# The second FFN of batches 2 to 7 as seven block products per 2x2 block, with weight sums read back from DRAM and VectorE held to the source's order

## The chip, the cores and the metric

The kernel runs on one core of one Trainium2 chip. The metric is the time of one execution on the device, in microseconds (us). In the profile PE is TensorE, which does the matrix products; PEld is its loading of the stationary operand; DVE is VectorE, ACT is ScalarE, POOL is GpSimd, and SP is SyncE, whose queue starts most DMAs. SBUF is the memory the engines compute from, PSUM the eight banks that PE writes its sums into, and DRAM the device's main memory.

## The reference, cut to what matters

Eight batches of 576 tokens go through an attention with 32 memory slots per head (8 heads of 64), and the result goes through a feed-forward network (FFN) of two large products. In all there are 4608 tokens, 512 model columns and 2048 hidden columns.

```python
a = softmax(phi)                                  # over the 32 slots
k_m = einsum('bhsm,bhsd->bhmd', a, k)             # and v_m likewise
attn = softmax(matmul(q, k_m.T) / sqrt(64))       # over the 32 slots
x = matmul(attn, v_m)  -> [4608, 512]
h = x @ w_in                                      # [4608, 2048]
g = h * (1.0 / (1.0 + np.exp(-h)))
return g @ w_out                                  # [4608, 512]
```

## The kernel before, in words

The first FFN is folded into the attention: `p_mm` (L592) multiplies `v_m` by `w_in` once per batch, 512 hidden columns at a time, and `ffn1` (L622) then multiplies that product by the attention weights. Every operand of the two large products is held as two parts, a rounded one and the rest of it (`hi` and `lo`), and each product is made of three: hi x hi, hi x lo and lo x hi.

**The loop.** For each batch `b` the main loop (L882) goes over 16 chunks `fc` of 128 hidden columns. One chunk is one slot. In a slot PE first does `ffn1`: twelve products with a moving operand of 288 tokens, into the PSUM tile `h`, which has one buffer. ACT applies silu to it (`silu`, L657): 512 tokens go into `g32`, and the 64 tokens left over go into `gleft`. DVE splits `g32` into `ghi` and `glo` (`split`, L646: a copy of 512 columns, then a subtraction of 512). Then come the events of this slot, and then `finish` (L874) does the second FFN of the slot before: `main_step` (L689) takes four tiles of 128 tokens, and for each of them `ffn2` (L671) does three products with a moving operand of 512 columns, which is all the model columns. So the order on PE is: first FFN of this slot, events of this slot, second FFN of the previous slot. Sums stay in the four `acc` banks for the whole batch and are copied out by `store` (L680) at its end. After every odd batch the left-over 64 tokens of two batches make one more tile of 128, done in four left steps (`left_step`, L695) of twelve products of 512 columns.

**The events** are the attention of the next batch `n`, spread over the slots of batch `b` by the tuple `at_slot` (L718), and the four `p_mm` of a batch. In the order of the tuple: `phi_max`; `phi_fold` and, half a slot later, `phi_sub`; `phi_exp`; `e_mm` (96 small products; half a slot or a slot from it the loads of `kv` and `q`); `e_tr`; `s_all` (scores, then transposes on DVE, of which two read columns beside `h`); `s_max` and `s_sub`; `s_exp`; `s_sum`; `s_norm`; `s_back` and `s_low` (the attention weights in two parts) with the load of the next `phi`. Each `p_mm` is followed by a copy on ACT and a subtraction on DVE (`p_split`, L612).

**What sets the order.** The context manager `in_order` (L98) ties each instruction of an engine to the one before it in the source. It holds PE throughout (L764), ACT from batch 1 on (L885), and SP in the opening and batch 0. DVE in batches 1 to 7 is placed by the scheduler of the framework.

Weights: `w_out` stands in SBUF as `wo_hi` and `wo_lo`, 16 chunks of 128 rows by 512 columns. `raw` is a pool of three buffers, through which weights come in and outputs go out; `cva` and `cva1` are two buffers that the weight conversion of batch 0 uses.

Of the kernel before, what the change touches and what calls it, by code (L numbers as in the profile page):

```python
# [48 lines left out]
def attn_ffn_kernel(  # L49
# [10 lines left out]
    const = ctx.enter_context(tc.tile_pool(name="const", bufs=1))  # L60
    sb = ctx.enter_context(tc.tile_pool(name="sb", bufs=2))
    ps = ctx.enter_context(tc.tile_pool(name="ps", bufs=1, space=bass.MemoryType.PSUM))

    kvn = const.tile([P, 2, 2, D], F32, name="kvn")
    ident = const.tile([P, P], F32, name="ident")
# [174 lines left out]
    def phi_max(b, ps_=(0, 1)):  # L240
        e, er = at[b]["e"], at[b]["er"]
        g = slice(ps_[0], ps_[-1] + 1)
        if "mx" not in at[b]:
            at[b]["mx"] = sb.tile([P, 2, P], F32, tag="mx", name="mx", bufs=1)
            at[b]["mt"] = sb.tile([P, 2, 2, P], F32, tag="g32", name="mt", bufs=2)
        mx, mt = at[b]["mx"], at[b]["mt"]
        nc.vector.tensor_tensor(mt[:, g], e[:, g, 0:2], e[:, g, 2:4], op=ALU.max)
        nc.vector.tensor_tensor(mx[:, g], mt[:, g, 0], mt[:, g, 1], op=ALU.max)
        for p in ps_:
            nc.vector.tensor_tensor(mx[rows(p), p], mx[rows(p), p], er[rows(p)], op=ALU.max)  # L250
# [62 lines left out]

    def e_mm(b):
        e, er, kvt, kr = (at[b][k] for k in ("e", "er", "kv", "kr"))
        pt = banks(b) if b < 2 else beside_h(KVW)
        turns = [(c, p) for c in range(FULLC) for p in range(2)]
        if b == 0:
            turns.sort(key=lambda t: t[1])
        for c, p in turns:  # L320
            for r in range(NR):
                nc.tensor.matmul(  # L322
                    pt[p][M * r : M * (r + 1), :KVW],
                    e[:, p, c, M * r : M * (r + 1)],
                    kvt[c][:, p, r],
                    start=c == 0, stop=False, skip_group_check=True,
                )
        for r in range(NR):
            for p in range(2):
                nc.tensor.matmul(  # L330
                    pt[p][M * r : M * (r + 1), :KVW],
                    er[rows(p), M * r : M * (r + 1)],
                    kr[rows(p), r],
                    start=False, stop=True, skip_group_check=True,
                )
        rs = [sb.tile([P, 1], F32, tag="rs", name="rs", bufs=2) for p in range(2)]
        for p in range(2):
            nc.vector.tensor_scalar(rs[p], pt[p][:, 2 * D : KVW], EPS, None, op0=ALU.add)
        for p in range(2):
            nc.vector.reciprocal(rs[p], rs[p])  # L340
        for p in range(2):
            src = pt[p][:, : 2 * D].rearrange("p (k d) -> p k d", k=2)
            if p == (b == 0):
                nc.scalar.activation(kvn[:, :, p], src, AF.Copy, scale=rs[p])
            else:
                nc.vector.tensor_scalar(kvn[:, :, p], src, rs[p], None, op0=ALU.mult)

    def e_tr(b):
        pt = beside_h(P)
        t = sb.tile([P, 2, NR, M], F32, tag="kvT", name=f"kvT{b}", bufs=2)  # L350
        for kind in range(2):
            nc.tensor.transpose(pt[kind], kvn[:, kind].rearrange("p g d -> p (g d)"), ident)  # L352
        nc.vector.tensor_copy(t[:, 0].rearrange("p r m -> p (r m)"), pt[0])
        nc.scalar.copy(t[:, 1].rearrange("p r m -> p (r m)"), pt[1])
        at[b]["kvT"] = t

    def s_all(b):
# [72 lines left out]

    def set_parts(b):
        for k, x in enumerate(("ahi", "alo")):
            at[b][x] = aparts[:, k, b % 2].rearrange("p (g s) -> p g s", g=2)

    def s_back(b, u):
        if "aT" not in at[b]:
            at[b]["aT"] = sb.tile([P, 2, S], F32, tag="att", name=f"aT{b}")
            set_parts(b)
        aT, ahi, sc = (at[b][k] for k in ("aT", "ahi", "sc"))
        c = slice(*u)  # L440
        for p in range(2):
            nc.vector.transpose(aT[:, p, c], sc[:, p, c])  # L442
        nc.scalar.activation(ahi[:, :, c], aT[:, :, c], AF.Copy)

    def s_low(b, u):
        aT, ahi, alo = (at[b][k] for k in ("aT", "ahi", "alo"))
# [139 lines left out]
    ALL = (0, S)  # L586

    pj = {}  # L590

    def p_mm(b, f, w, low=True):  # L592
        j = f // JW
        if f % JW == 0:
            pj[b, j] = [pparts[:, k, j % 2].rearrange("p (g f) -> p g f", g=2) for k in range(2)]
        hi, lo = pj[b, j]
        c = slice(f % JW, f % JW + w)
        bg = bgtile()
# [47 lines left out]
    def split(g32, steps=(0, 1), gs=None):  # L646
# [7 lines left out]
            last_split.append(nc.vector.tensor_tensor(glo, g32, ghi, op=ALU.subtract))  # L654
        return gs

    def silu(b, fc, h):  # L657
        g32 = sb.tile([P, MAIN], F32, tag="g32", name="g32", bufs=2)
        w = MAIN // 2
        nc.scalar.activation(g32.rearrange("p (h f) -> p h f", h=2), h[:, :, :w], AF.Silu)  # L660
# [8 lines left out]
    acc = {}  # L669

    def ffn2(gs, cs, fc, key):  # L671
        ghi, glo = gs
# [5 lines left out]
            )  # L678

    def store(key, rows, last=False):  # L680
        o = sb.tile([P, DMODEL], F32, tag="raw", name="o", bufs=RAWB)
        a = acc.pop(key)
        nc.scalar.activation(o, a, AF.Copy)  # L683
        at_ = 0
# [15 lines left out]

    events = {}

    def ev(b, slot, fn, *a):
# [2 lines left out]
    for b in range(B):  # L708
        n = b + 1
        if b == 0:  # L710
            for j in range(2, DFF // CW):
                ev(b, 2 * j - 1.5, p_mm, b, j * CW, CW)
        else:
            for j in range(1, NJ):
                ev(b, 4 * j - 3, p_mm, b, j * JW, JW)
        if n == B:
            continue
        at_slot = (4, 5, 6, 7.5, 9, 9.5, 11.5, 12.5, 13, 13.5, 13.5, 14) if b == 0 else (1, 2, 3, 5, 9, 10, 10, 11, 12, 13, 13, 14)  # L718
# [24 lines left out]
        ev(b, se, s_exp, n, ALL)  # L743
        ev(b, ss, s_sum, n, ALL)
        ev(b, sn, s_norm, n, ALL)
        ev(b, sk, s_back, n, ALL)
        ev(b, sk, s_low, n, ALL)
        if n + 1 < B:
            ev(b, sk, load_phi, n + 1)
        ev(b, 14, p_mm, n, 0, JW)  # L750
# [123 lines left out]
    def finish(tiles):  # L874
        if prev is None:
            return
        if prev[0] == "main":
            main_step(prev[1], prev[2], prev[3], tiles)
        elif tiles[0] == 0:
            left_step(prev[1], prev[2], prev[3])  # L880

    for b in range(B):  # L882
        if b == 1:
            whole.close()
            ctx.enter_context(in_order(ACT))  # L885
        for fc in range(NFC):
# [22 lines left out]
            prev = ("main", b, fc, gs)  # L909
        if b % 2:  # L910
            for n in range(NLS):
                gs = split(gleft[:, n * NI : (n + 1) * NI].rearrange("p c f -> p (c f)"))
                finish((0, 1, 2, 3))
                prev = ("left", b, n, gs)
    finish((0,))
# [55 lines left out]
```

## Time and profile before

| what | value |
|---|---|
| time, median of 3 runs | 701.71 us |
| the runs | 701.3, 701.71 and 702.42 us |
| span of the profiled execution, first to last instruction | 700.3 us |
| PE busy | 689.4 us, 4924 products |
| DVE busy | 365.4 us, 665 instructions |
| ACT busy | 259.0 us, 456 instructions |
| POOL busy | 0.7 us, 6 instructions |
| DMA | 60.15 MB, 86 GB/s in the mean |

The profiled execution's own time is not listed apart from its span; the runs' times lie 1.0 to 2.1 us above that span. Busy time is the union of an engine's instructions. Products on PE are pipelined: each is listed with about 0.3 to 0.4 us, but they start closer together than that, so the price of one is the distance between two starts.

### The profile page before, as it was taken

The page shows a single profiled execution, that of the slowest core. Times are in us where ns is not written, and L with a number is a line of the kernel's source. Part 1 is how long each engine was busy: PE and PEld are TensorE (multiplying, and loading weights), DVE is VectorE, ACT ScalarE, POOL GpSimd, SP SyncE. Part 2 cuts the span into 40 slices and gives each one's busy share as a digit, 9 for nine tenths or more (in the row PEclk, how much of TensorE's full clock was granted, in tenths as well). Part 3 has the DMA queues.
Part 4 walks back from the last instruction along what each step waited for, and adds up shares of the span by engine and source line. Part 5 has one row for each costly group of instructions (what it writes and reads, how often), then busy time and mean ns, then how long its engine had stood idle before and what let it go on. Part 6 is the DMA issues. An engine that isn't in the chain of part 4 may idle for free.

```text
span 700.3 us, 11773 instructions
## 1 busy us (share of the span) xinstructions
PE 689.4 (98%) x4924; PEld 562.4 (80%) x4924; DVE 365.4 (52%) x665; ACT 259.0 (37%) x456; POOL 0.7 (0%) x6
## 2 busy tenths in 40 slices
PE   7999999999999999999999999999999999999997
PEld 3578777888888888888888888888888888888886
DVE  4898797435654256534636346542564525623322
ACT  3879584422424224421423314342241413431211
POOL 0000000000000000000000000000000000000000
PEclk9999999999999999999999999999999999999999
DMA  9995752212201221132110311112121000010002
GB/s 334 317 338 187 254 212 95 78 61 68 92 19 46 92 68 44 52 137 69 35 61 16 137 56 47 61 54 83 68 80 31 1 1 1 1 61 1 1 0 76
DMA packets 25445, 60.15 MB, mean 86 GB/s; under 512 B 2096, under 2 KB 10416, under 8 KB 25392
## 3 DMA queue, kind: packets, MB, share of 16 engines
q1 hardware_dynamic: 24448, 56.63, 22.8%
q10 hardware_dynamic: 944, 2.77, 1.1%
q8 instruction: 39, 0.64, 0.4%
q14 instruction: 14, 0.11, 0.1%
HBM read 49.95 MB, written 9.44 MB: 85 GB/s over the span
## 4 chain that ended last, share of the span: by engine, by line
PE 84%; DVE 2%; issue 0%; ACT 0%; ACTq 0%
PE acc L676 45%; PE h L637 25%; PE accleft L676 6%; PE bg L602 4%; PE h L322 2%; PE bg L367 1%; DVE wo_lo L176 0%; DVE raw L172 0%; PE h L330 0%; PE h L352 0%; DVE aparts L448 0%; DVE aT L442 0%; DVE gparts L654 0%; DVE sc L415 0%; DVE smx L411 0%
## 5 line engine op out<-in xcount | busy, mean ns | idle before, releaser
L676 PE MATMUL acc<-wo_hi,gparts 128*128 128x512 f32 x1024 | 341.8, 395 | 0.1
L676 PEld LDWEIGHTS acc<-wo_hi,gparts 128*128 128x128 f32 x1024 | 192.0, 188 | 52.7 <-issue 6.6
L637 PEld LDWEIGHTS h<-aparts,pparts 128*128 128x128 f32 x1524 | 214.0, 188 | 14.4 <-issue 2.1
L637 PE MATMUL h<-aparts,pparts 128*128 128x288 f32 x1524 | 223.3, 295 | 0.7 <-ACT aparts L581 0.4
L660 ACT ACTIVATE g<-h 128x512 f32<-128x512 f32 x127 | 76.0, 599 | 345.9 <-PE h L637 180.3
L676 PE MATMUL acc<-wo_lo,gparts 128*128 128x512 f32 x512 | 200.8, 392 | 0.7 <-DVE wo_lo L176 0.6
L652 DVE CAST gparts<-g 128x512 fp32r<-128x512 f32 x128 | 54.4, 425 | 260.0 <-ACT g L660 260.0
L676 PEld LDWEIGHTS acc<-wo_lo,gparts 128*128 128x128 f32 x512 | 96.1, 188 | 18.4 <-DVE wo_lo L176 1.9
L654 DVE TENSOR_TENSOR gparts<-g,gparts 128x512 fp32r<-128x512 f32 x128 | 88.2, 689 | 10.3
L618 DVE TENSOR_TENSOR pparts<-bg,pparts 128x1024 fp32r<-128x1024 f32 (+1 forms) x36 | 39.7, 1102 | 5.4 <-ACT pparts L616 5.0
L676 PE MATMUL accleft<-wo_hi,gparts 128*128 128x512 f32 x128 | 40.6, 389 | 0.0
L616 ACT ACTIVATE pparts<-bg 128x1024 fp32r<-128x1024 f32 (+1 forms) x36 | 33.6, 932 | 14.8 <-PE bg L602 14.8
L602 PE MATMUL bg<-win,kvT 64*32 64x512 f32 (+1 forms) x576 | 35.8, 554 | 0.0
L676 PEld LDWEIGHTS accleft<-wo_hi,gparts 128*128 128x128 f32 x128 | 24.0, 188 | 4.9
L662 ACT ACTIVATE gleft<-h 128x64 f32<-128x64 f32 x127 | 27.8, 219 | 0.0
L683 ACT ACTIVATE o<-acc 128x512 f32<-128x512 f32 x32 | 19.2, 600 | 21.8 <-PE acc L676 10.6
L676 PE MATMUL accleft<-wo_lo,gparts 128*128 128x512 f32 x64 | 24.9, 389 | 0.0
L660 ACT ACT_TABLE_LOAD x14 | 18.0, 1283 | 14.2 <-issue 13.6
L652 DVE CAST gparts<-gleft 128x512 fp32r<-128x512 f32 x16 | 6.8, 427 | 20.7 <-PE accleft L676 12.2
L168 ACT ACTIVATE raw<-raw 128x1024 int32<-128x1024 uint32 (+1 forms) x16 | 16.8, 1048 | 0.0
L322 PEld LDWEIGHTS h<-kv,phi 128*32 128x32 f32 x384 | 10.2, 110 | 5.0 <-ACT gleft L662 5.0
L676 PEld LDWEIGHTS accleft<-wo_lo,gparts 128*128 128x128 f32 x64 | 12.0, 188 | 2.4
(139 smaller groups left out, 365.0 us busy)
## 6 DMA issues: line engine op xcount, KB each, us to landing
kv<-in_kv SPq DMA_DIRECT2D x28, 516.0 KB, 5.9
q<-in_q SPq DMA_DIRECT2D x16, 576.0 KB, 5.7
out<-o SPq DMA_DIRECT2D x32, 256.0 KB, 2.1
raw<-in_w_in SPq DMA_DIRECT2D x14, 512.0 KB, 6.6
raw<-in_w_out SPq DMA_DIRECT2D x6, 1024.0 KB, 5.5
phi<-in_phi SPq DMA_DIRECT2D x7, 576.0 KB, 3.8
kv<-in_kv ACTq DMA_DIRECT2D x4, 516.0 KB, 6.8
kr<-in_kv SPq DMA_DIRECT2D x7, 258.0 KB, 6.4
```

Of the source, the lines that this page charges most:

```text
L168: nc.scalar.activation(r, low, AF.Copy, scale=2.0**-29)
L322: nc.tensor.matmul(pt[p][M * r : M * (r + 1), :KVW], e[:, p, c, M * r : M * (r + 1)], kvt[c][:, p, r], start=c == 0, stop=False, skip_grou ...
L602: nc.tensor.matmul(bg[M * r : M * (r + 1), p, :w].rearrange("p (k f) -> p k f", f=P), kvT[D * p : D * (p + 1), 1, r], win[D * p : D * (p + ...
L616: nc.scalar.activation(hi[:, :, c], bg[:, :, :w], AF.Copy)
L618: nc.vector.tensor_tensor(lo[:, :, c], bg[:, :, :w], hi[:, :, c], op=ALU.subtract)
L637: nc.tensor.matmul(h[:, hf, :HALF], wt[:, p, fs], a[:, p, hf * HALF : (hf + 1) * HALF], start=n[hf] == 0, stop=n[hf] == 5, skip_group_chec ...
L652: nc.vector.tensor_copy(ghi, g32)
L654: last_split.append(nc.vector.tensor_tensor(glo, g32, ghi, op=ALU.subtract))
L660: nc.scalar.activation(g32.rearrange("p (h f) -> p h f", h=2), h[:, :, :w], AF.Silu)
L662: i = nc.scalar.activation(gleft[:, fc, o : o + LEFT].rearrange("p (h f) -> p h f", h=2), h[:, :, w:HALF], AF.Silu)
L676: nc.tensor.matmul(acc[key], gt[:, cs], wt[:, fc], start=fc == 0 and n == 0, stop=fc == NFC - 1 and n == 2)
L683: nc.scalar.activation(o, a, AF.Copy)
```

## The change

The change concerns batches 2 to 7. In them the loop's 16 slots are no longer 16 chunks for all tokens, but two halves `t` of the tokens times eight pairs `j` of chunks. A slot handles 256 tokens (two tiles of 128), two chunks and all 512 model columns, which is a 2x2 matrix of blocks times a 2x2 matrix of blocks. Those eight block products are replaced by seven (the scheme of Strassen in Winograd's form), which need sums of blocks of `g` and of `w_out` first and sums of the products afterwards. Each block product has a moving operand of 256 columns and again three parts, so a slot has 21 products of 256 columns in the place of 12 of 512.

- **Sums of `g`** (`forms`): per slot, DVE makes four sums, copies four blocks to their rounded part and subtracts seven blocks; ACT copies three blocks. Silu writes into `gbuf`, which has one buffer in these batches, since the sums are in it too.
- **Sums of `w_out`** (`w_forms`): in batch 1 POOL makes them, ACT and DVE split them, and a DMA writes them to DRAM (1 MB for each of the eight pairs). Three of the four sums per pair are read back, 256 KB each, into a ring of four places just before use (`ring_load`, three per slot). The fourth replaces the right half of `wo_hi` and `wo_lo` (`t1_load`).
- **Sums of the products** (`st_out`): after each half, ACT copies two banks out and DVE does seven additions of 256 columns, three of them with an operand in PSUM.
- **Left-over tokens**: `left_st` does 24 products of 256 columns per left step; at its end ACT copies and DVE adds twice.
- **Order**: DVE is held to the source's order from batch 2 on. The events of batches 2 to 6 have slots of their own, and `s_low` is cut in two halves, the second of which runs in slot 1 of the next batch.

```diff
+    gbuf = const.tile([P, 2 * MAIN], F32, name="gbuf")
...
-        pt = banks(b) if b < 2 else beside_h(KVW)
+        pt = beside_h(KVW) if b == 2 else banks(b)
...
+    def s_high(b, u):
         c = slice(*u)
...
+        nc.scalar.activation(at[b]["ahi"][:, :, c], at[b]["aT"][:, :, c], AF.Copy)
...
+    def w_forms(j, step):
...
+        if step == 0:
...
+            nc.gpsimd.tensor_tensor(f, as_f32(wo_hi[:, c]), as_f32(wo_lo[:, c]), op=ALU.add)
+            b11, b12, b21, b22 = (f[:, k, q * Q : (q + 1) * Q] for k in range(2) for q in range(2))
+            nc.gpsimd.tensor_tensor(b11, b12, b11, op=ALU.subtract)
+            nc.gpsimd.tensor_tensor(b12, b22, b12, op=ALU.add)
+            nc.gpsimd.tensor_tensor(b22, b22, b11, op=ALU.add)
+            nc.gpsimd.tensor_tensor(b21, b22, b21, op=ALU.subtract)
+            return
+        f = at[0]["forms", j].rearrange("p k (q f) -> p (k q) f", q=2)
+        nc.scalar.activation(ring[0][:, :, :Q], f, AF.Copy)
+        nc.vector.tensor_tensor(ring[0][:, :, Q:], f, ring[0][:, :, :Q], op=ALU.subtract)
+        load(saved[j], as_f32(ring[0]))
...
+    def ring_load():
+        u = next(asked, None)
+        if u is not None:
+            j, k = uses[u]
+            load(as_f32(ring[0][:, u % 4]), saved[j][:, k])
...
+    def forms(b, t, j, h):
...
+        nc.scalar.activation(gbuf[:, :MAIN].rearrange("p (i f) -> p i f", i=2), h[:, :, :w], AF.Silu)
+        o = b % 2 * LEFT + t * (LEFT // 2)
+        nc.scalar.activation(gleft[:, 2 * j : 2 * j + 2, o : o + LEFT // 2], h[:, :, w:HALF], AF.Silu)
+        hi, lo = form_high[j % 2], form_low[j % 2]
+        nc.scalar.activation(hi[:, :3], g[:, 1:4], AF.Copy)
+        nc.vector.tensor_tensor(
+            g[:, 4:6], g[:, :1].broadcast_to([P, 2, P]), g[:, 1:3], op=ALU.subtract
+        )
+        nc.vector.tensor_tensor(g[:, 6], g[:, 1], g[:, 5], op=ALU.subtract)
+        nc.vector.tensor_tensor(g[:, 7], g[:, 3], g[:, 6], op=ALU.subtract)
+        nc.vector.tensor_copy(hi[:, 3:], g[:, 4:])
+        nc.vector.tensor_tensor(lo, g[:, 1:], hi, op=ALU.subtract)
+        return hi, lo
...
+    HIGH, LOW = ((0, 0), (0, 1)), ((1, 0),)
...
+    def st_step(b, t, j, part):
+        if j == 0:
+            sums[:] = [ps.tile([P, DMODEL], F32, tag="acc", name=f"sum{i}", bufs=NI) for i in range(4)]
...
+        held = ((0, 0, 0, b11), (0, 1, 2, b21), (1, 0, 6, b22), (1, 1, 4, b12))
+        for terms in (HIGH, LOW):
+            for bank, place, k, w in held:
+                product(bank, place, part, k, w, terms)
+        for bank, place, k in ((2, 0, 5), (2, 1, 3), (3, 0, 1)):
+            r = ring[0][:, next(used) % 4]
+            product(bank, place, part, k, (r[:, :Q], r[:, Q:]), HIGH + LOW)
+            ring_load()
+        if j == NP - 1:
+            st_out(b, t)
+
+    def st_out(b, t):
...
+        for i in range(2):
+            nc.scalar.activation(o[:, i], sums[i], AF.Copy)
...
+        add(u2, sums[2][:, :Q], c11)
+        add(u3, sums[2][:, Q:], u2)
+        add(c11, c11, c12)
+        add(c12, u2, c22)
+        add(c12, c12, c21)
+        add(c21, u3, sums[3][:, :Q], ALU.subtract)
+        add(c22, u3, c22)
...
+        else:
+            ev(b, 0, p_mm, b, (3 if b > 2 else 2) * JW, JW)
+            if b == 2:
+                ev(b, 2, p_mm, b, 3 * JW, JW)
+            else:
+                ev(b, 1, s_high, b, SECOND)
+                ev(b, 1, s_low, b, SECOND)
...
+            else (1, 2, 3, 5, 9, 10, 10, 11, 12, 13, 13, 14) if b == 1
+            else (0, 1, 3, 5, 6, 7, 7, 9, 10, 11, 11, 13)
...
+        else:
+            for j in range(3):
+                ev(b, 10 + 2 * j, p_mm, n, j * JW, JW)
...
+        if b == 2:
+            ctx.enter_context(in_order(DVE))
+        for s in range(NFC if b > 1 else 0):
...
+            t, j = divmod(s, NP)
+            h = ffn1s(b, t, j)
+            part = forms(b, t, j, h)
+            for part_ in range(2):
+                for fn, a in events.pop((b, s + part_ / 2), []):
+                    fn(*a)
+            finish(range(NI))
+            prev = ("st", b, t, j, part)
```

Not shown are new homes for some buffers, `ffn1s` (the first FFN for one half of the tokens and two chunks, twelve products of 288 tokens as before), `product` (the three products of a block), `left_split` and `left_st`. In the events of batch 1 stand also the two steps of `w_forms` for each of the eight pairs, from slot 2 to slot 13.5.

More of the change, by code (lines that the diff above doesn't have):

```diff
@@ L594, in p_mm @@
         if f % JW == 0:
-            pj[b, j] = [pparts[:, k, j % 2].rearrange("p (g f) -> p g f", g=2) for k in range(2)]
+            p_home(b, j)
         hi, lo = pj[b, j]
@@ L655, in split @@
         return gs
+    half = iter(range(1 << 30))
     def silu(b, fc, h):
-        g32 = sb.tile([P, MAIN], F32, tag="g32", name="g32", bufs=2)
+        g32 = gbuf.rearrange("p (n f) -> p n f", n=2)[:, next(half) % 2]
         w = MAIN // 2
@@ L667, in silu @@
         return g32
-    acc = {}
+    acc, homes = {}, []
     def ffn2(gs, cs, fc, key):
@@ new lines, in product @@
+    def product(bank, place, part, k, w, first):
+        hi, lo = part
+        whi, wlo = w
+        for gt, wt in first:
+            gt, wt = (hi, lo)[gt], (whi, wlo)[wt]
+            key = bank, place
+            nc.tensor.matmul(
+                sums[bank][:, place * Q : (place + 1) * Q], gt[:, k], wt,
+                start=bank not in begun, stop=True, skip_group_check=True,
+            )
+            begun.add(bank)
+    sums, begun = [], set()
+    HIGH, LOW = ((0, 0), (0, 1)), ((1, 0),)
```

167 lines of the change are left out of this document (142 added, 25 removed).

## The prediction, made before the changed kernel ran

> **What bounds the kernel now.** I read the page first, for shares and clock, then the chain of waits in order of time, for the price of each piece, and then the other engines in one batch. The page:
>
> ```profile
> span 700.3 us, 11773 instructions
> ...
> PE 689.4 (98%) x4924; PEld 562.4 (80%) x4924; DVE 365.4 (52%) x665; ACT 259.0 (37%) x456; POOL 0.7 (0%) x6
> ...
> PEclk9999999999999999999999999999999999999999
> ...
> PE 84%; DVE 2%; issue 0%; ACT 0%; ACTq 0%
> ```
>
> PE is the bound, at full clock, with next to no waits. The chain gives its prices:
>
> ```profile
> 189.78 8.16 PE accleft L676 x36
> ...
> 306.59 1.58 PE h L637 x12
> 308.17 2.74 PE acc L676 x12
> ...
> 345.57 1.02 PE bg L602 x16
> ...
> 351.12 5.46 PE acc L676 x24
> 356.58 8.16 PE accleft L676 x36
> ```
>
> A slot is 1.58 us of first FFN (12 products of 288 columns, 131.7 ns each) and 2.73 us of second FFN (12 of 512; 5.46/24 = 227.5 ns). Two batches with their left tile are 356.58 - 189.78 = 166.8 us. DVE's half share is a mean; a batch and the handing over within a slot show what it has to do and when:
>
> ```profile
> 273.20:356.60 83.40, 83.40 (x603) 69.47 (x602) 41.92 (x80) 29.39 (x54) 0.00 (x0) 1.00 0.19 66
> ```
>
> ```profile
> 308.27 0.60 ACT L660 ACTIVATE g<-h 128x512 f32<-128x512 f32 x1 [3.72 <-PE h L637]
> ...
> 308.90 0.43 DVE L652 CAST gparts<-g 128x512 fp32r<-128x512 f32 x1 [3.97 <-ACT g L660]
> ...
> 309.43 0.69 DVE L654 TENSOR_TENSOR gparts<-g,gparts 128x512 fp32r<-128x512 f32 x1
> ```
>
> In 83.4 us DVE works 41.92. In a slot it starts 0.73 us after the first FFN's end (308.90 - 308.17), works 1.1 us and then waits; PE needs its result only 2.73 + 1.58 us after that end. So today all of DVE is covered.
>
> **Change 1: the products.** 21 of 256 columns take the place of 12 of 512. No row has 256 columns. A line through the two sizes gives 131.7 - 32 x (227.5 - 131.7)/224 = 118 ns; the bounds are half of the 512 price (114) and the whole 288 price (131.7). I take 118, since 256 lies beside 288. Then the second FFN of a slot is 2.48 us and not 2.73: 0.25 saved, 96 times, is 24.0. The left tile pays: 96 x 118 ns for 48 x 227.5 ns, 0.4 more, three times, 1.3. PE alone thus gains **22.7 us** (at 131.7 ns it would lose 9).
>
> **Change 2: the sums of g on DVE.** Prices:
>
> ```profile
> L654 DVE TENSOR_TENSOR gparts<-g,gparts 128x512 fp32r<-128x512 f32 x128 | 88.2, 689 | 10.3
> ...
> L618 DVE TENSOR_TENSOR pparts<-bg,pparts 128x1024 fp32r<-128x1024 f32 x28 | 34.1, 1220 | 2.5 <-ACT pparts L616 2.2
> ...
> L683 ACT ACTIVATE o<-acc 128x512 f32<-128x512 f32 x32 | 19.2, 600 | 21.8 <-PE acc L676 10.6 <-DMA out<-o 9.8
> ...
> L247 DVE TENSOR_TENSOR mt<-phi 128x512 f32<-128x512 f32 x7 | 4.8, 691 | 0.2
> ...
> L250 DVE TENSOR_TENSOR mx<-mx,phi 64x128 f32<-64x128 f32 x16 | 4.5, 284 | 0.2
> ...
> L248 DVE TENSOR_TENSOR mx<-mt 128x256 f32<-128x256 f32 x7 | 2.9, 418 | 0.0
> ```
>
> Per slot: 0.42 (256 columns), twice 0.28 (128), the copy 0.43, the subtraction of 896 columns 1.09 (between 0.69 and 1.22), and some 0.2 between dependent instructions (0.1 between the two DVE rows above): 2.7 us where there were 1.1. Beside a PE slot of 1.58 + 2.48 = 4.06 us this still fits by itself. It ends 0.73 + 2.7 = 3.45 us after the first FFN's end. PE asks for the low parts at the ninth product of the next block step, 2.48 + 1.58 + 8 x 0.118 = 5.0 us after it. Less 0.15 for the signal the **slack is 1.4 us**.
>
> **Change 3: DVE in the source's order.** The sums of slot s+1 now queue behind all events of slot s, and PE waits for those sums; `gbuf` and `h` have one buffer each, so nothing runs further ahead. The lag of DVE grows in each slot by 2.7 + events - PE's slot; what exceeds the slack is a stall of PE. The events' prices:
>
> ```profile
> 250.78 1.31 DVE L374 STREAM_TRANSPOSE sc<-bg 128x512 f32<-128x512 f32 x2
> 252.01 0.34 DVE L376 STREAM_TRANSPOSE sc<-h 128x64 f32<-128x64 f32 x2
> 252.38 1.35 DVE L411 TENSOR_REDUCE smx<-sc 128x36 f32<-128x1152 f32 x1
> 253.76 1.36 DVE L415 TENSOR_TENSOR sc<-sc,smx 128x1152 f32<-128x1152 f32 x1
> ...
> 262.27 1.35 DVE L423 TENSOR_REDUCE ssm<-sc 128x36 f32<-128x1152 f32 x1 [1.37 <-ACT sc L419]
> ...
> 264.30 1.36 DVE L429 TENSOR_TENSOR sc<-sc,ssm 128x1152 f32<-128x1152 f32 x1
> ...
> 267.17 0.77 DVE L442 STREAM_TRANSPOSE aT<-sc 128x576 f32<-128x576 f32 x1
> ```
>
> ```profile
> 284.37 0.45 DVE L275 STREAM_TRANSPOSE mxt<-mx 128x256 f32<-128x256 f32 x1
> ...
> 285.18 1.21 DVE L618 TENSOR_TENSOR pparts<-bg,pparts 128x1024 fp32r<-128x1024 f32 x1
> ...
> 290.03 0.41 DVE L652 CAST gparts<-g 128x512 fp32r<-128x512 f32 x1
> ...
> 290.47 0.29 DVE L304 TENSOR_TENSOR phi<-phi,am 64x128 f32<-64x128 f32 x1
> ```
>
> `phi_fold` with `phi_sub` is 290.76 - 284.37 less the two strangers in it (1.21, 0.41): 4.8 us. `phi_max` is 0.69 + 0.42 + 2 x 0.28 = 1.7, a `p_mm` costs DVE 1.2 and PE 1.0, `st_out` 7 x 0.42 = 2.9, the second half of `s_low` 0.8.
>
> - *Slots 0 and 1.* Batches 3 and 5, with `st_out` of the batch before: slot 0 is 2.7 + 1.2 + 1.7 + 2.9 = 8.5 against 5.1 on PE; slot 1 is 2.7 + 0.8 + 4.8 = 8.3 against 4.06. The lag is 7.6, the stall 6.2, and some 0.4 more from lag brought along: 6.6. Batches 4 and 6 come after a left tile (2.83 for 2.48 on PE, 0.84 for 2.9 on DVE): 1.0 + 4.2 - 1.4 = 3.8. Batch 2 has neither `s_low` nor additions there, and a `p_mm` in slot 2: 1.4. Batch 7 has no attention: 0.4. Sum 13.2 + 7.6 + 1.4 + 0.4 = **22.6**.
> - *Slot 7.* The scores' transposes read beside `h`, and the next first FFN writes `h`. They end 3.45 + 1.65 + 0.1 = 5.2 us after slot 7's first FFN. PE's own work until then:
>
> ```profile
> 326.80 1.09 PE L367 MATMUL bg<-q,kvT 64*32 64x288 f32 x32
> ...
> 328.00 0.50 PE L676 MATMUL acc<-wo_hi,gparts 128*128 128x512 f32 x1
> ```
>
>   1.2 + 2.48 = 3.7. Stall 1.5, five batches: **7.5**.
> - *Slots 8 to 14.* `st_out` in 8 (+1.6), maximum and subtraction in 9 (2.74: +1.4), sum and normalising in 11 (3.4: +2.0), the way back in 13 (some 3: +1.7), and -1.1 in 10, 12 and 14, whose `p_mm` also widens the slack by 1.0. Stalls 0.6, 0.9 and 0.5; five batches: **10**.
> - *Left tiles.* The last block step follows the one before without a first FFN between (1.5, in batches 3 and 5), and left step 1 waits for its split, which queues behind `st_out`: copy 0.7, additions 2.9, split 1.2 are 4.9 with signals, against 2.8 on PE: 2.1, three times. **9.3**.
>
> Stalls: 49.4 us. ACT has room (29.39 of 83.4 busy); its copies in `st_out` (0.60 each) are in the sums above.
>
> **Change 4: DMAs and batch 1.** The ring takes 0.77 MB per slot of about 4 us, some 190 GB/s. A place has to be refilled within about 3.7 us, a slot less the run-out of the product that frees it (0.3). SP's queue is passed by the `kv` load:
>
> ```profile
> 301.98 3.04 SPq L87 DMA_DIRECT2D kv<-in_kv  x4
> ```
>
> ```profile
> 303.50:310.50 7.00, 7.00 (x45) 6.01 (x36) 2.12 (x8) 1.08 (x3) 0.00 (x0) 1.00 0.85 323
> ```
>
> It starts under `e_mm` (slot 5) and fills the engines for 7 us at 323 GB/s, until some 8.5 us after its start. Ring loads that queue behind it land some 10 us after that start, and are wanted from 8.8 us on: late by 0 to 1.3 us, in batches 2 to 5. I take 0.5 each: 2. The queue's order is not in this trace: should the `phi` load stand in it, waiting for DVE, ahead of ring loads, those would be late by up to 3.5 us per batch (below). In batch 1 eight steps add 1.2 us each on DVE and 1.0 on ACT beside half-idle engines, and POOL runs five instructions per step, 1.2 + 4 x 0.42 = 2.9 us if it were as fast as DVE. Bounds 0 (all in DVE's idle 41 us) and 8 (split after split delayed past its slack); I take 1, near the free end. The Trainium skill (SBUF - State Buffer, "Who interferes with whom") says that a DVE instruction with two SBUF inputs and a GpSimd one that reads SBUF block each other for the whole instruction. POOL is idle in every window here, so no run shows it; by that rule the term lies in the upper half of its bounds, the sum at 734 to 738.
>
> **Sum**: 700.3 - 22.7 + 49.4 + 2 + 1 = 730.0 of span, and the runs' median is 1.4 above the span: **731 us**.
>
> **Rivals.**
> 1. *DVE's lag stays covered, PE remains the bound: faster.* For it: DVE's total per two batches, 2 x 41.92 + 32 x 1.6 + 4 x 2.9, is 147 us, under PE's 166.8 - 32 x 0.25 = 159. Against: order, not the total. It decides at stalls of 22.7 us, 4.1 per batch; below that it is faster. Wholly covered: 701.7 - 22.7 + 3 = 682.
> 2. *The loading of the stationary operand binds at 256 columns, 131.7 ns.* PE +31, but slots 0.29 longer save some 18 of the stalls: 744. Against: at 288 columns the price lies on a line with that of 512.
> 3. *Ring loads stand behind waiting DMAs in SP's queue.* 3.5 us, batches 2 to 5: 745.
> 4. *The long wait cools PE.* In slots 2 and 3 of batches 3 to 6 PE stands some 3.2 to 3.7 us at a stretch. Cold, it is slow though the page's clock reads full:
>
> ```profile
> 1.36 4.12 PE L79 MATMUL idle<-ident 128*128 128x512 bf16 x10 [1.36 <-POOL ident masks.py:199]
> ...
> 18.62 2.97 PE L79 MATMUL spare<-ident 128*128 128x512 bf16 x13
> ```
>
>   The first ten start 0.40 us apart, the later ones 0.22. Four stretches of 4.1 us at half speed cost 8: 739. The Trainium skill (TensorE: Matmul & The Clock Gate, "What's actually happening") has the rate halved after a whole idle window of about 3.4 us; the first rows agree with a cold start, and the waits here would be at its edge.
>
> **How the numbers follow.** Forecast 0.62, rival 1 0.26 (a chain with so many links can be mis-sized by half), rivals 2, 3 and 4 together 0.12. 0.2% is what a measurement can tell. Faster 0.25, within 0.2% 0.04, slower 0.71. The forecast's own range is 713 to 748 (stalls a quarter either way, and the open terms); the whole range takes in most of rival 1 and most of the others: 684 to 750.
>
> **What would show it.** Right: DVE at 560 us or more, products of 256 columns 118 ns apart, PE waiting for the subtraction or copy of the sums for 3 us or more around slots 2 and 3 of each batch 3 to 6, first FFN of slot 8 waiting for the transposes beside `h`, left step 1 waiting for a split. Wrong: PE waits of under 20 us in batches 2 to 7, or most of them named after DMAs.

## The result, and the profile after

| | before | after |
|---|---|---|
| median of 4 runs each, same chip | 701.5 us | 761.05 us (758.63 to 761.8) |
| ratio to before | | 1.084, 95% interval 1.082 to 1.086 |
| profiled span | 700.3 us | 756.8 us |

The change made the kernel 8.4% slower. The sign and the largest cause were forecast; 731 us was too low by 30, and 761 lies above the range (684 to 750).

The page of the kernel after, first engines and clock, then the chain that ended last:

```profile
span 756.8 us, 15051 instructions
...
PE 697.9 (92%) x5932; PEld 603.2 (80%) x5932; DVE 554.4 (73%) x1056; ACT 306.5 (40%) x565; POOL 50.6 (7%) x46
...
POOL 0000030677100000000000000000000000000000
...
PE 40%; DVE 27%; DMA 11%; issue 4%; POOL 3%; ACT 3%; DVEq 0%; SPq 0%; ACTq 0%
```

PE carried 84% of the chain before and carries 40% now; DVE has 27%, and DMA 11%, nearly all of it ring loads. POOL, idle before, works through batch 1 (slices 6 to 11). In the kernel after, L783 is the first FFN, L814 the block products, L794 the silu, L799 to L803 the sums of `g`, L804 the copy and L805 the subtraction behind them; L378 are the transposes beside `h`. PE's longest totals of waiting in this kernel (total, times, longest):

```profile
PE sum L814 <- DMA ring<-forms: 16.3, 22, 1.4
PE h L783 <- DVE sc L378: 6.9, 5, 1.7
PE sum L814 <- DVE aparts L804: 6.0, 5, 2.1
PE sum L814 <- DVE gparts L805: 3.9, 9, 0.5
```

The largest named waiter is one that I had priced at 2 us. Where the time went by stage shows in the windows (columns: length, then busy time and instructions of PE, PEld, DVE, ACT and POOL, the clock, the DMA share, GB/s). Before, cut at the first FFN of batch 1 and of batch 2:

```profile
0.00:108.20 108.20, 101.92 (x821) 72.37 (x821) 87.36 (x146) 76.21 (x115) 0.70 (x6) 1.00 0.75 267
108.20:197.80 89.60, 89.34 (x627) 74.05 (x628) 45.71 (x86) 29.09 (x53) 0.00 (x0) 1.00 0.21 76
197.80:700.30 502.50, 498.17 (x3479) 415.96 (x3477) 232.38 (x434) 153.73 (x288) 0.00 (x0) 1.00 0.14 49
```

After, cut at the same points of the work:

```profile
0.00:111.50 111.50, 103.55 (x821) 73.49 (x822) 91.04 (x147) 76.29 (x115) 7.94 (x11) 0.98 0.74 262
111.50:211.70 100.20, 93.10 (x644) 75.03 (x643) 65.69 (x95) 37.88 (x62) 42.66 (x35) 0.98 0.46 169
211.70:756.80 545.10, 501.22 (x4471) 454.67 (x4469) 397.71 (x816) 192.32 (x388) 0.00 (x0) 1.00 0.61 184
```

The span grew by 56.5: **13.9** before batch 2 begins (211.7 - 197.8, forecast 1) and **42.6** from there on (545.1 - 502.5, forecast 28.7 = -22.7 + 49.4 + 2). So half of the miss of 27 stands before batch 2, which does not even contain the new products.

The second half splits cleanly. Taking each start of a product against the regular spacing (132 ns after one of 288 columns, 119 after one of 256; what exceeds it by over 60 ns is a wait) gives 67.1 us of waits in batches 2 to 7. Without them 545.1 is 478.0. The same sum over the experiments below:

| from batch 2 on, us | length | waits | without waits | waits at high parts | low parts | ring and banks | `h` | at half clock |
|---|---|---|---|---|---|---|---|---|
| after | 545.1 | 67.1 | 478.0 | 11.2 | 8.2 | 34.8 | 9.9 | 3.4 |
| e1, nothing read back | 534.7 | 57.1 | 477.6 | 18.9 | 11.7 | 9.5 | 13.4 | 17.0 |
| e4, DVE's order free | 530.6 | 53.1 | 477.5 | 3.7 | 3.7 | 36.4 | 9.0 | 6.8 |
| e5, attention spread | 530.7 | 51.9 | 478.8 | 3.4 | 1.6 | 35.7 | 8.1 | 6.8 |
| e6, two of three read back | 536.2 | 58.6 | 477.6 | 20.6 | 11.5 | 10.0 | 13.0 | 20.4 |
| e7, no sums of `g` | 526.6 | 47.9 | 478.7 | 4.2 | 1.5 | 37.7 | 2.0 | 6.8 |
| e8, nearly all left out | 494.0 | 16.8 | 477.2 | 6.6 | 3.0 | 1.6 | 2.2 | 0 |
| e12, best whole kernel | 522.2 | 43.6 | 478.6 | 3.3 | 1.7 | 26.9 | 6.9 | 3.4 |

What is left without waits is 477 to 479 in every kernel, 502.5 - 478 = 24.5 us less than the whole stretch of before. But by the same rule before has 2.9 us of such gaps itself: 28 times the second product of a slot comes 0.1 us late. Like for like the products save **21.6 us**, where I forecast 22.7. Everything else is waiting. In the kernels of the table that same 0.1 us stands in the column of the high parts, 3.4 to 6.6 us of it in each, behind a wait or behind the small products of the attention. What e4 and e5 have left there is this, and next to no wait for DVE. (The columns leave out small places. The last one is the time that the clock record has at a half; half of it is lost, and counts as waits here. Before has none of it in these batches.)

A piece of PE's timeline in batch 3 shows three kinds of wait (start, length, in brackets the idle time and its releaser):

```profile
311.66 0.50 PE L814 MATMUL sum<-ring,aparts 128*128 128x256 f32 x2 [0.98 <-DMA ring<-forms]
...
312.12 1.75 PE L783 MATMUL h<-aparts,pm 128*128 128x288 f32 x12
313.71 0.28 PE L814 MATMUL sum<-wo_hi,aparts 128*128 128x256 f32 x1
...
314.06 0.28 PE L814 MATMUL sum<-wo_lo,aparts 128*128 128x256 f32 x1
316.48 0.39 PE L814 MATMUL sum<-wo_hi,aparts 128*128 128x256 f32 x1 [2.14 <-DVE aparts L804]
...
317.71 0.50 PE L814 MATMUL sum<-wo_hi,gparts 128*128 128x256 f32 x2 [0.49 <-DVE gparts L805]
```

Products of 256 columns start 0.117 us apart, as forecast. The first four need only what ACT copied; the fifth stands until DVE's copy of the sums (L804) is there, then the low parts are late too. The start of batch 3 on DVE shows why:

```profile
300.55 1.22 DVE L631 TENSOR_TENSOR pparts<-bg,pparts 128x1024 fp32r<-128x1024 f32 x1
301.68 0.68 DVE L249 TENSOR_TENSOR mt<-phi 128x512 f32<-128x512 f32 x1
...
303.47 0.43 DVE L851 TENSOR_TENSOR x<-sum,oo 128x256 f32<-128x256 f32 x1
...
306.12 0.42 DVE L851 TENSOR_TENSOR oo<-x,oo 128x256 f32<-128x256 f32 x1
306.46 0.42 DVE L799 TENSOR_TENSOR gbuf<-gbuf 128x256 f32<-128x256 f32 x1
...
313.81 0.68 DVE L303 TENSOR_TENSOR phi<-phi,am 128x512 f32<-128x512 f32 x1
314.50 0.29 DVE L306 TENSOR_TENSOR phi<-phi,am 64x128 f32<-64x128 f32 x1
314.82 0.43 DVE L799 TENSOR_TENSOR gbuf<-gbuf 128x256 f32<-128x256 f32 x1
...
316.00 0.43 DVE L804 CAST aparts<-gbuf 128x512 fp32r<-128x512 f32 x1
```

A `p_mm`, the maximum of `phi` and the seven additions of `st_out` stand in a row in front of the sums that PE wants, without a gap. Some 8 us later it is the subtraction of `phi` (L303, L306), and the copy behind it ends at 316.43, 0.05 us before PE goes on. It is the queue that the prediction wrote down for slots 0 and 1.

### The profile page after: what moved, and what is told of

It reads as the page before. It is cut to its first block, busy times and chain, and to the rows that moved or that the text cites. A ratio compares the mean times of both kernels' runs of the same rounds, so it can differ in the third digit from the quotient of the medians.

```text
span 756.8 us, 15051 instructions
## 1 busy us (share of the span) xinstructions
PE 697.9 (92%) x5932; PEld 603.2 (80%) x5932; DVE 554.4 (73%) x1056; ACT 306.5 (40%) x565; POOL 50.6 (7%) x46
## 4 chain that ended last, share of the span: by engine, by line
PE 40%; DVE 27%; DMA 11%; issue 4%; POOL 3%; ACT 3%; DVEq 0%; SPq 0%; ACTq 0%
PE sum L814 17%; PE h L783 11%; DMA ring<-forms 11%; DVE gparts L805 5%; PE acc L691 3%; PE lsum L814 3%; DVE oo L851 2%; PE bg L615 2%; DVE aparts L804 2%; PE h L650 2%; DVE gbuf L799 2%; POOL wf L747 1%; PE bg L324 1%; DVE gbuf L802 1%; DVE gbuf L803 1%
## 5 line engine op out<-in xcount | busy, mean ns | idle before, releaser
L794 ACT ACTIVATE gbuf<-h 128x512 f32<-128x512 f32 x96 | 57.4, 597 | 267.9 <-PE h L783 145.3
L814 PE MATMUL sum<-ring,aparts 128*128 128x256 f32 x576 | 115.4, 292 | 20.3 <-DMA ring<-forms 16.3
L805 DVE TENSOR_TENSOR gparts<-gbuf,aparts 128x896 fp32r<-128x896 f32 x96 | 104.9, 1092 | 12.8 <-DVE aparts L804 0.5
L814 PEld LDWEIGHTS sum<-ring,aparts 128*128 128x128 f32 x576 | 88.6, 191 | 30.7 <-DMA ring<-forms 24.2
L799 DVE TENSOR_TENSOR gbuf<-gbuf 128x256 f32<-128x256 f32 x96 | 40.6, 423 | 96.9 <-ACT gbuf L794 96.7
L814 PE MATMUL sum<-wo_hi,aparts 128*128 128x256 f32 x384 | 100.1, 293 | 6.0 <-DVE aparts L804 6.0
L814 PE MATMUL sum<-wo_lo,aparts 128*128 128x256 f32 x384 | 96.1, 282 | 0.0
L814 PEld LDWEIGHTS sum<-wo_hi,aparts 128*128 128x128 f32 x384 | 72.6, 189 | 24.8 <-issue 13.0
L783 PE MATMUL h<-aparts,pm 128*128 128x288 f32 x576 | 84.5, 296 | 6.9 <-DVE sc L378 6.9
L691 PE MATMUL acc<-wo_hi,gparts 128*128 128x512 f32 x256 | 87.6, 402 | 2.4 <-DVE gparts L667 2.2
L783 PE MATMUL h<-aparts,pparts 128*128 128x288 f32 x576 | 84.4, 295 | 0.8 <-ACT gleft L796 0.8
L783 PEld LDWEIGHTS h<-aparts,pm 128*128 128x128 f32 x576 | 78.4, 189 | 7.9 <-issue 7.7
L814 PE MATMUL sum<-ring,gparts 128*128 128x256 f32 x288 | 80.8, 280 | 0.0
L783 PEld LDWEIGHTS h<-aparts,pparts 128*128 128x128 f32 x576 | 78.1, 188 | 1.6 <-ACT gleft L796 1.5
L814 PEld LDWEIGHTS sum<-wo_lo,aparts 128*128 128x128 f32 x384 | 72.9, 190 | 0.0
L814 PE MATMUL sum<-wo_hi,gparts 128*128 128x256 f32 x384 | 64.1, 289 | 4.0 <-DVE gparts L805 3.9
L650 PEld LDWEIGHTS h<-aparts,pparts 128*128 128x128 f32 x372 | 52.7, 192 | 13.0 <-ACT kvT L356 3.0
L691 PEld LDWEIGHTS acc<-wo_hi,gparts 128*128 128x128 f32 x256 | 48.5, 191 | 17.2 <-DVE gparts L667 4.8
L814 PEld LDWEIGHTS sum<-wo_hi,gparts 128*128 128x128 f32 x384 | 53.0, 192 | 6.8 <-DVE gparts L805 6.3
L814 PEld LDWEIGHTS sum<-ring,gparts 128*128 128x128 f32 x288 | 54.4, 189 | 0.0
L691 PE MATMUL acc<-wo_lo,gparts 128*128 128x512 f32 x128 | 51.1, 399 | 1.0 <-DVE wo_lo L178 0.9
```

The lines of the kernel that those rows point to most:

```text
L650: nc.tensor.matmul(h[:, hf, :HALF], wt[:, p, fs], a[:, p, hf * HALF : (hf + 1) * HALF], start=n[hf] == 0, stop=n[hf] == 5, skip_group_chec ...
L691: nc.tensor.matmul(acc[key], gt[:, cs], wt[:, fc], start=fc == 0 and n == 0, stop=fc == NFC - 1 and n == 2)
L783: nc.tensor.matmul(h[:, i, :HALF], wt[:, p, f : f + P], a[:, p], start=n == 0, stop=n == 5)
L794: nc.scalar.activation(gbuf[:, :MAIN].rearrange("p (i f) -> p i f", i=2), h[:, :, :w], AF.Silu)
L799: nc.vector.tensor_tensor(g[:, 4:6], g[:, :1].broadcast_to([P, 2, P]), g[:, 1:3], op=ALU.subtract)
L805: nc.vector.tensor_tensor(lo, g[:, 1:], hi, op=ALU.subtract)
```

## The experiments

**e1: nothing is read back.** The ring is filled once.

```diff
-        if u is not None:
+        if u is not None and u < 4:
```

> Leaves out the reading back of the weight sums after the first four: the ring's places keep what they hold, and 284 of 288 loads of 256 KB are gone. Theory A (of the 35 us of PE waits at ring products some 28 are ring loads that land after their one slot of time): they go, and what is left is DVE's order with batch 1 as it is, 761 - 28 + some 8 of DVE lag that the ring waits had covered, 735 to 745. Rival B (the ring waits only stand where DVE's lag would stop PE anyway): 755 or more.

Measured 750.1 us (ratio 1.069, 1.067 to 1.070): 11 less, between A and B. The ring's waits fell from 34.8 to 9.5 (bank waits), but high parts rose from 11.2 to 18.9 and `h` from 9.9 to 13.4. The waits of this kernel:

```profile
PE sum L814 <- DVE aparts L804: 12.0, 7, 3.4
PE h L783 <- DVE sc L378: 6.9, 5, 1.7
```

Most of the ring's waits had only stood where PE would have waited for DVE a little later. And the waits for DVE are now in one piece, up to 3.4 us, and longer idling lowers the clock: 17.0 us at a half, where the kernel after has 3.4. The window from batch 2 on has it in its clock column:

```profile
212.00:746.60 534.60, 497.97 (x4471) 457.64 (x4469) 397.77 (x816) 191.97 (x388) 0.00 (x0) 0.98 0.14 48
```

The ring's net price is 10 to 11, not 2 and not 25; with the clock's 8.5 against 1.7 taken out of both it would be 17.

**e2: the sums of the weights on DVE** instead of POOL, in all five lines of `w_forms`.

```diff
-            nc.gpsimd.tensor_tensor(f, as_f32(wo_hi[:, c]), as_f32(wo_lo[:, c]), op=ALU.add)
+            nc.vector.tensor_tensor(f, as_f32(wo_hi[:, c]), as_f32(wo_lo[:, c]), op=ALU.add)
```

> The sums of w_out are made by DVE instead of POOL, everything else the same. Batches 0 and 1 are 14 us longer than in the kernel before. Theory A (POOL blocks DVE instructions, and ACT stands in its order waiting for POOL's sums): DVE gets 23 us more work in batch 1, half of which it has free, but nothing blocks: 748 to 753. Rival B (the 1 MB stores and the one ring buffer make batch 1 longer): 758 to 763.

Measured 751.0 us (1.070, 1.068 to 1.072): A. Batch 2 now begins at 200.8 and not at 211.7, although the same 40 operations were added to the engine that is the scarce one later. The edit takes away both things that theory A names, the blocked DVE and ACT's wait for POOL, so it does not tell them apart.

**e3: the same sums half a slot earlier**, still on POOL.

```diff
-                ev(b, 1.5 * j + 2, w_forms, j, 0)
+                ev(b, 1.5 * j + 1.5, w_forms, j, 0)
```

> POOL starts each sum half a slot earlier, right behind the step that frees its buffer, so that ACT waits less for it; POOL does as much beside DVE as before. If ACT's waits for POOL (20.7 us in six waits) are what makes batch 1 longer: 752 to 755. If it is DVE blocked while POOL runs: 759 to 763.

Measured 761.1 us (1.086, 1.082 to 1.090): no change, but the edit did not move POOL either. Already in the kernel after, seven of POOL's eight steps start as soon as DVE's subtraction (L756) has freed their one buffer `wf`, less than 0.1 us behind it, and in e3 POOL waits for that subtraction for the same 39.9 us and ACT for POOL for 20.8 us (20.7 in the kernel after). So e3 says nothing between its two theories. The trace of the kernel after shows both at work. The first, in the chain that ended last:

```profile
149.53 2.40 POOL wf L747
...
154.83 0.74 POOL wf L752
...
155.59 1.07 ACT ring L755
...
156.69 1.24 DVE ring L756
...
157.99 2.52 POOL wf L747
```

POOL's five operations, ACT's copy and DVE's subtraction follow one another round the one buffer. ACT is held in order, so what stands behind its copy waits with it, and PE's three longest waits between 112 and 196 us name such work of ACT:

```profile
PE h L650 <- ACT gleft L677: 2.2, 1, 2.2
PE h L650 <- ACT kvT L356: 2.1, 1, 2.1
PE h L324 <- ACT gleft L677: 1.4, 1, 1.4
```

For the last two, ACT had stood 3.0 and 2.9 us before its copy, waiting for POOL. The second thing shows where the timelines of DVE and POOL lie side by side:

```profile
139.00 0.42 DVE L665 CAST gparts<-gbuf 128x512 fp32r<-128x512 f32 x1
139.52 2.68 DVE L667 TENSOR_TENSOR gparts<-gbuf,gparts 128x512 fp32r<-128x512 f32 x1
```

```profile
139.16 2.49 POOL L747 TENSOR_TENSOR wf<-wo_hi,wo_lo 128x1024 f32<-128x1024 f32 x1 [2.43 <-DVE ring L756]
```

The subtraction of the split, elsewhere 0.69 us, lasts until POOL's sum is done, and goes on for 0.55 us after it. PE's waits over 0.15 us in batch 1 and just before it, 9.2 us in all, name ACT for 5.7 and DVE for 3.5 (before has 0.3 there). Two stretches of 3.4 us at half clock, from 107.2 and from 189.2, come on top. POOL is also slow itself:

```profile
L747 POOL TENSOR_TENSOR wf<-wo_hi,wo_lo 128x1024 f32<-128x1024 f32 x8 | 20.4, 2550 | 138.2 <-DVE raw L174 98.2 <-DVE ring L756 39.9
L752 POOL TENSOR_TENSOR wf<-wf 128x256 f32<-128x256 f32 x8 | 8.2, 1023 | 0.6
```

**e4: DVE no longer held to the source's order.**

```diff
-        if b == 2:
-            ctx.enter_context(in_order(DVE))
```

> DVE is not held to the source's order in batches 2 to 7; the framework's scheduler places its instructions. Theory A (the source's order makes the sums of g queue behind the attention; some 35 us of PE waits at the copies, the low parts, h and the banks): 735 to 750. Rival B (DVE's total and the ring loads set the time, whatever the order): 755 to 765. The scheduler's own order may also be worse: over 765.

Measured 744.6 us (1.061, 1.059 to 1.063): A, 16.5 less. High and low parts fall from 19.4 to 7.4 us; the ring's 36 stay.

**e5: the steps of the next batch's attention spread out.** Most begin one to two slots later, and `phi_fold` is split over three.

```diff
-            else (0, 1, 3, 5, 6, 7, 7, 9, 10, 11, 11, 13)
+            else (1, 2, 5, 6, 7, 8, 8, 9, 10, 11, 11, 13)
...
-                ev(b, sub, phi_fold, n, i)
-        ev(b, sub + 0.5, phi_sub, n)
+                ev(b, sub + i * (b > 1), phi_fold, n, i)
+        ev(b, sub + (2.5 if b > 1 else 0.5), phi_sub, n)
```

> In batches 2 to 6 the attention's first part is spread over DVE's idle slots (maximum in slot 1, the three steps of the fold in 2, 3 and 4, the subtraction in 4.5, exponential 5, e_mm 6, e_tr 7, scores 8); the rest stays. Theory A (DVE's lag by the source's order, 6.6 and 3.8 us around slot 2): the waits at copies and low parts in slots 1 to 3, 11 us in the changed kernel, go, less what ring loads then show: 748 to 753. Rival B (ring waits take their place in full): 757 or more.

Measured 743.0 us (1.055, 1.049 to 1.062): 18 less, more than A gave it. The four runs lie between 736.3 and 746.0, so the size is good to about 5 us. High and low parts are down to 5.0 with DVE still in order: it was what stood in the queue, not the rule of order by itself.

**e6: two reads per slot and not three.** The third product takes a block that is held.

```diff
-    RING = (3, 1, 2)
+    RING = (3, 1)
```

> Leaves out the reading of one of three weight sums (that product uses a block that is held): two loads per slot for four places, so a place has two slots to be filled in, and 96 of 288 loads are gone. Theory A (ring loads are late because two of three places have one slot, about 4.0 us, and a load lands 3.5 to 4.3 us after its place is free): as without reloading, 748 to 752. Rival B (the DMA engines' rate is short): a third of that gain, 756 to 759.

Measured 750.2 us (1.068, 1.067 to 1.070), the same as with no reads at all: A. A third less data removes the whole price; a place then has two slots, and no load lands less than 2.5 us before its use. The smaller traffic has a part in it, which this run doesn't separate: from release to landing a load takes 3.4 to 3.5 us in the middle here. This is how the ring's refill looks over all 284 loads of the kernel after: of the three uses in a slot one is refilled for two slots later (release to next use 8.9 us in the middle), the two others for the next slot (5.0 and 5.3 in the middle, 3.9 and 4.0 in the tightest tenth). From release to the last of a load's 16 completions 3.5 to 4.6 us pass. In the tight places window and load are the same figure, and 57 of these loads land less than 0.15 us before their use.

**e7: no sums of `g`.** The three instructions are left out, the copy takes four of the plain blocks.

> Leaves out the three instructions that make the sums of g (the copy takes other blocks): DVE's chain in a slot is some 1.1 us shorter, its slack 1.1 us wider and its lag 1.1 us smaller per slot. Theory A (DVE's lag is the larger part of the loss): 728 to 740, with ring waits left. Rival B (ring loads set the pace once DVE is out of the way): 745 or more.

Measured 742.2 us (1.056, 1.052 to 1.061): 19 less, between A and B. The waits for high and low parts mostly go (5.7 of 19.4 left), the ring's remain (37.7).

**e8: what PE alone would give.** No reading back, no sums of `g`, one of eight sums of the weights.

> PE's own price: leaves out the reading back of weight sums, the sums of g and seven of eight weight sums in batch 1. What is left of the loss is h in slot 7, the additions at the end of each half, and the left tiles. Theory A (21 products of 256 columns at 118 ns gain 22.7 us on PE): 690 to 698. Rival B (the block products cost PE more than that, by waits of their own): 705 or more.

Measured 698.0 us (0.995, 0.993 to 0.997): A, and the only kernel below the one before. From 201.7 on its window reads:

```profile
201.70:695.70 494.00, 481.56 (x4471) 448.35 (x4469) 303.30 (x528) 192.58 (x388) 0.00 (x0) 1.00 0.15 52
```

8.5 us less than before's 502.5, with 16.8 of waits still in it where before has 2.9: a PE saving of 22.4, so the 21.6 are real.

**e9: e2 and e5 together.**

> The sums of the weights made on VectorE (which alone gave -10) and the later steps of the next batch's attention spread over the slots (which alone gave -18). A, the two touch different stretches (batch 1; batches 2 to 6): the savings add up, 761 - 10 - 18 = 733 us, 728 to 738. B, what the spread saved was in part the same time, for instance the DVE backlog that batch 1 hands to batch 2: 740 us or more. Neither reaches the kernel before (701.5).

Measured 736.5 us (1.051, 1.049 to 1.052): A, they add up. (The profiled execution took 2283.5 us, with products more than twice their usual length; it is left out, so that e9 has no trace to read.)

**e10: e9 with DVE's order free.**

> The same two, and DVE no longer held to the source's order from the third batch on. A, order and placement are two cures for one thing (DVE late with the high and low parts, of which the trace with the spread alone still shows 5.0 us of PE waits): not more than 5 us below the kernel with the two, so 727 to 733 us. B, they cure different waits: the free order's own -16.5 is added, 715 to 720 us.

Measured 741.9 us (1.057, 1.055 to 1.058): neither; 5 slower than e9. With the places well chosen the source's order is the better one. The trace has more waits for low parts than e5 (8.5 for 1.6) and 39.9 at the ring; 17.0 us of it ran at half clock, which costs 8.5. Which exchange of instructions causes that I did not follow.

**e11: e9 with the ring loads issued by GpSimd.**

```diff
-            load(as_f32(ring[0][:, u % 4]), saved[j][:, k])
+            nc.gpsimd.dma_start(as_f32(ring[0][:, u % 4]), saved[j][:, k])
```

> The two, and the loads of the ring are issued by GpSimd instead of SyncE, whose queue also holds the loads of the next batch's attention that wait for their tiles. With the spread alone 35.7 us of PE waits stand at the ring's products and bank positions, 12.7 of them in slot 6, where the load of q is issued. A, the ring loads stand behind a waiting load in SyncE's queue (my rival 3): the 12.7 us go, and some of the rest: 715 to 722 us. B, the loads need 3.5 to 4 us to land and have one slot of 4.06: no change against the two alone (within 4 us, about 733). C, GpSimd issues a transfer more slowly than SyncE: above 740 us.

Measured 756.2 us (1.075, 1.071 to 1.079): C. The ring's line among the waits and among the DMA issues:

```profile
PE sum L814 <- DMA ring<-forms: 33.7, 52, 2.5
...
ring<-forms POOLq DMA_DIRECT2D x288, 256.0 KB, 3.9
```

The landing is the 3.9 us of SyncE's queue; what grew is the time from release to issue (0.41 to 0.75 us in the middle, by place, where it was 0.03 to 0.22). Slot 6 has 14.5 us of waits at the ring, where e5 had 12.7, so these are not a place in SyncE's queue. In 46 loads of the kernel after a load of `q` or `kv` was under way: they landed in 5.0 us in the middle, the other 242 in 3.8.

**e12: e9 with the ring's products between the low terms of the held ones.**

```diff
-        for terms in (HIGH, LOW):
-            for bank, place, k, w in held:
-                product(bank, place, part, k, w, terms)
+        for bank, place, k, w in held:
+            product(bank, place, part, k, w, HIGH)
+        low = iter(held)
         for bank, place, k in ((2, 0, 5), (2, 1, 3), (3, 0, 1)):
+            if k != 5:
+                for _ in range(2):
+                    bk, pl, kk, w = next(low)
+                    product(bk, pl, part, kk, w, LOW)
```

> The two, and the three products from the ring stand between the held products' low terms, at places 9, 14 and 19 of the 21 instead of 13, 16 and 19, so that a place of the ring has 23 instead of 21 products (0.24 us more) from its release to its next use. A, the loads miss their window by little (landing 3.5 to 4.0 us against 4.06): of the 35.7 us some 10 to 15 go, 718 to 724 us. B, they miss it by more, because they are held up in SyncE's queue: within 4 us of the two alone. C, the first low product stands 0.35 us earlier behind the high ones, so that the low parts come too late: above 736 us.

Measured 723.0 us (1.031, 1.030 to 1.032): A. 0.24 us more of window per load saves 13.4 us in all; the ring's waits went from 35.7 (e5, since e9 has no trace) to 26.9, which is 8.8 of it. It is the best kernel that does the whole work, 38 us below the one after and 3.1% above the one before.

## Why the prediction was right, and where it was wrong

- **Products: right.** 0.117 to 0.12 us apart, 21.6 us saved against 22.7. Rival 2 (131.7 ns) fell with the first rows. ("No row has 256 columns" overlooked 128 products of `p_mm`; these start eight at a time 7 ns apart and give no price for a product by itself.)
- **Sums on DVE: right.** 2.7 us per slot forecast; in a free stretch of the chain after, from the end of the first FFN (583.46) to the end of the last sum (586.94) it is 3.48 against the forecast 3.45:

```profile
583.48 0.61 ACT gbuf L794
...
584.11 0.44 DVE gbuf L799
...
585.29 0.44 DVE aparts L804
...
585.85 1.09 DVE gparts L805
```

- **DVE's queue in the source's order: right, mechanism and size.** Without the ring's loads it stands alone: e1 has 57.1 us of waits and e6 58.6. Of these the half clock makes 8.5 and 10.2, which leaves 48.6 and 48.4 at the least (a product that is slowed while DVE is late anyway costs nothing), against the forecast 49.4. The places are those forecast: around slots 2 and 3 (in e1 17 us stand in slot 3, at the products made from slot 2's sums), and the first FFN of slot 8 behind the transposes (8.0 us in the kernel after for 7.5). e4 and e5 cure it from two sides. Rival 1 needed less than 22.7 us of stalls and is dead.
- **Ring loads: the term "I take 0.5 each: 2" was wrong.** Its measured net price is 10 to 11 (e1, e6). I had the window right ("about 3.7 us") and asked only who else queues or transfers, not how long an ordinary load of the ring takes. For the places with one slot it takes 3.5 and 4.0 us from release to landing in the middle, so that it has next to no margin even without a load of `q` or `kv` beside it. How much of that the ring's loads cost each other isn't shown: the fastest of the 288 landed 2.9 us after its issue. The page of before had three rows that bear on it (KB, median us to landing), a store of 256 KB and loads of 576 and 258 KB, which the working left out; at 2.1 to 6.4 us they don't settle the price, but they put 3.7 us in doubt:

```profile
out<-o SPq DMA_DIRECT2D x32, 256.0 KB, 2.1
...
phi<-in_phi SPq DMA_DIRECT2D x7, 576.0 KB, 3.8
...
kr<-in_kv SPq DMA_DIRECT2D x7, 258.0 KB, 6.4
```

  Rival 3 had another mechanism, the place in the queue, which e11 speaks against.
- **Batch 1: the term "I take 1, near the free end" was wrong, and so was its bound of 8.** It was 13.9. POOL was priced like DVE, 2.9 us per step; its five lines, two of which stand above, sum to 50.0 us, 6.25 per step. That slowness reaches PE by two ways: ACT, in order, waits for POOL's sums (a wait that the prediction did not have at all), and a DVE instruction with two operands in SBUF lasts until POOL's ends. e2 takes 10.9 of the 13.9 away, so POOL's making of the sums is the cause; how it divides between the two ways stays open, since e3 changed neither. Some 3 us stay even in e2 and e12, where batch 2 begins at 200.8 and 200.7; their cause is open too, but it hardly lies in the eight steps, since e8 with one step begins batch 2 at 201.7. The Trainium skill (SBUF — State Buffer, "Who interferes with whom") had the block; the trace agrees, 2.68 us for 0.69. The prediction quoted it and took a value against it. The Trainium skill (GPSIMD Engine Reference, "Elementwise — side-by-side cycle accounting") had the speed too: it measures a two-input add at 1.96 times DVE's time. An estimate from that makes 2.4 us of DVE's 1.22; the shortest of L747 took 2.38. Neither entered the sum.
- **Clock: rival 4 was right as a mechanism, beside the forecast and not in its place.** After a wait the granted clock fell to a half for just 3.4 us. Windows around the one in batch 5:

```profile
500.00:503.20 3.20, 1.46 (x12) 1.25 (x11) 2.85 (x9) 0.00 (x0) 0.00 (x0) 1.00 0.28 93
503.20:506.60 3.40, 3.13 (x16) 2.83 (x15) 2.37 (x6) 2.47 (x5) 0.00 (x0) 0.50 0.02 5
506.60:510.00 3.40, 3.40 (x29) 3.40 (x29) 1.28 (x2) 3.37 (x5) 0.00 (x0) 1.00 0.74 227
```

  Sixteen products instead of 29 in 3.4 us: half of it, 1.7 us, is lost. The kernel after has three of these before its end, 5 us (1.7 of it in batches 2 to 7), and in those batches e1 and e6 have five and six times 3.4 us (8.5 and 10.2), where I had priced 8. The Trainium skill (TensorE: Matmul & The Clock Gate, "What's actually happening") gives 3.4 us for the window, and the trace agrees; it asks for an idle window, and here PE had worked 1.46 of the 3.2 us before.

Added up, as net prices: products -21.6 (forecast -22.7), waits that stay without the ring's loads 54 (57.1 in e1 less the 2.9 that before has too; forecast 49.4, with nothing for the clock), the ring's loads 10 (2), batch 1 13.9 (1): 56.4, against the span's growth of 56.5. Of the miss of 27, 13 are batch 1, 8 the ring and 8.5 the clock; the products add 1, and DVE's queue without the clock takes off 4 (46 for 49.4). This is priced by leaving the ring out. In the kernel after itself the clock is 1.7, and the ring some 15 over its forecast.

## What to carry to other kernels

Fewer products on PE pay only while everything that feeds them still fits into the shorter slot: here 22 us were saved, and the sums, their order and their transport cost 78 (54 + 10 + 14). When work goes to an idle engine or a ring, price the operation on that engine and the landing of one ordinary transfer before asking who competes; and check what that engine blocks and who waits for it in order. Where one engine works in order, place its bursts first (18 us here) and free its order only if that fails.

## What the runs showed of the hardware that was not expected

- A GpSimd operation makes a DVE subtraction of two SBUF operands last until it ends: 2.68 us for 0.69.
- A GpSimd sum with two inputs takes 2.4 us for 128x1024 when undisturbed and 0.73 for 128x256; 2.55 and 0.83 to 1.02 in the mean here.
- A 256 KB load of the ring landed 3.9 us after its issue in the middle of 288, from SyncE's queue and from GpSimd's alike; from SyncE's it was 3.8 without and 5.0 beside a load of `q` or `kv`, and 2.9 the fastest. GpSimd's issue came 0.4 to 0.6 us later after the release.
- The clock falls to a half for 3.4 us although PE was busy 1.46 of the 3.2 us before.
